# Two channel pieces placed earlier, and three ScalarE steps reordered, in a fused attention and Fourier-mix kernel

## The chip, the cores and the metric

The kernel runs on one core of a Trainium2 chip. A core has five engines with a queue each: TensorE (PE, matmuls and transposes, with its weight loads shown as PEld), VectorE (DVE), ScalarE (ACT), GpSimd (POOL) and SyncE (SP, which here only starts DMA transfers). Each engine works through its own instructions in the order in which the program gives them; engines wait for one another by semaphores. The metric is the device time of one execution in microseconds (us); lower is better.

## The reference

Two blocks follow one another. The first is an attention with a threshold, over 8 batches and 8 heads of 576 rows with 64 columns; the second mixes with a two-dimensional Fourier transform and ends in a normalised two-layer product.

```
scores = (q @ k.T) / 8
thresh = max(scores, rows) - tau
scores = where(scores >= thresh, scores, -1e9)
attn   = exp(scores - max) / (sum + 1e-9)
x      = (attn @ v), heads side by side: (8, 576, 512)
u      = x + real(fft over rows and columns of x)
un     = (u - mean(u)) / sqrt(var(u) + 1e-6)
out    = u + relu(un @ w_ch1) @ w_ch2        # 512 -> 2048 -> 512
```

The weights `w_ch1` and `w_ch2` arrive as 64-bit floats and are converted to 32 bits on the core.

## The kernel before, in words

**Steps.** A pair of heads is handled in five steps, four with 128 query rows of both heads and a fifth with the last 64 rows of both. With four pairs in a batch that gives 20 steps in a batch and 160 in all. They are numbered here from 0; step `i` belongs to pair `n = i // 5` and has `t = i % 5`. Steps 0 to 19 are the first batch (`step`, L1499), steps 20 to 39 the second (`second_batch`, L1647), and one loop runs steps 40 to 159 (L1724 on). All of it is unrolled, and the order of the program is written out by hand: what is called first is queued first on its engine.

**What a step does.** `scores(i)` puts the scores of 128 rows into PSUM: eight matmul records, at L440, or four at L446 in the fifth step of a pair. `softmax(i)` takes the row maxima (DVE, L461), the exponentials (ACT, L469), the threshold (ACT, L473), applies the threshold and sums (DVE, L477), and forms the inverse sums (`inverse`, DVE, L385 and L388). There are two score buffers, so the scores of step `i + 1` wait for the threshold operation of step `i`. `transposed_weights(i - 1)` transposes the weights of the step before on TensorE (L587, L590, L605), and ACT copies them from PSUM (L593 or L597, then L607 or L609). In the first two batches the inverse sums are not multiplied into the weights: `spread_inverse(i)` lets ACT spread them over 128 columns as `rec` (L509; in the fifth step of a pair a small copy, L504, comes first), TensorE transposes `rec` along with the weights (L590), and they are applied to the product with the values. `weighted_values` is that product (L636), twice per pair: in the second batch its first part is in the steps with `t = 2` and its second part in the steps with `t = 0` of the next pair. `scale_q` (ACT, L399) scales the queries of the next pair in the steps with `t = 2`, and `prep_pair` (DVE, L408 to L411) transposes queries and keys in the steps with `t = 3`, after which SP loads the next ones.

**Conversion.** `convert` turns 64-bit weights into 32-bit ones in stages spread over two steps: DVE (L296, L299), ACT (L304, L307), DVE (L311), POOL (L316), ACT (L318) and POOL (L319). The first batch converts `w_ch1`, the second `w_ch2` after the table `PLAN`, up to two pieces in a step.

**Channel work.** The two-layer product is done in groups of 512 rows. Group 0 is `channels`: 16 pieces of the first layer (each eight matmul records into one PSUM bank at L902, then a Relu, on ACT at L907 for an even piece and on DVE at L909 for an odd one), four loads of rows with their statistics (`rows.load`, L851 to L863), and then the second layer, four blocks of 16 matmuls each (L926) that is given out two matmuls at a time. `rows.factors()` takes the square roots (L874) and then a dummy exponential (L877), so that ACT loads its table of functions twice. Every two matmuls of the second layer also move on `w1_forms`, which stores pieces of `w_ch1` to memory (SP) and combines them (DVE, L970).

**The budget.** `fill()` is called three times in a step. Each call adds `per_slot` to `budget` and then runs pieces as long as `spent < budget`; every piece reports its cost in columns. `start_batch(0)`, in step 20, sets

```
keep = 4 * BT * NJ * DM // 128 if b == 0 else 3 * 7 * 2048
per_slot = (todo - spent - keep) / (3 * per_batch)
```

`keep` is what is left for the third batch: here 4 * 512 * 16 * 512 / 128 = 131072 columns. `todo` is 19240 for the mixing of the first batch and 264192 for group 0, so `per_slot` is 2539.3. In steps 23 to 39 the order of the program is: scores, softmax, `fill`, transposes of the step before, the ACT stage of the conversion, `fill`, `prep_pair` if due, `fill`, product with the values if due, `scale_q` if due, `spread_inverse`.

**PSUM.** All of these banks but the scores' come from one ring of four, tag `mm`; a new tile waits for the last reader of the bank that it is given.

Of the kernel before, what the change touches and what calls it, by code (L numbers as in the profile page):

```python
# [28 lines left out]
def _repeated(ap, n):  # L29

    return bass.AP(
        tensor=ap.tensor,
        offset=ap.offset,
        ap=[list(ap.ap[0]), list(ap.ap[1]), [0, n]],
    )
# [12 lines left out]
def kernel(  # L48
# [14 lines left out]
    DM = H * D  # L63
# [5 lines left out]
    NJ = HID // 128  # L69
# [7 lines left out]
    BT = 512  # L77
# [318 lines left out]
    def scale_q(n):  # L396

        raw = loaded[n][0]
        nc.scalar.activation(out=raw[:, :], in_=raw[:, :], func=ACT.Copy, scale=q_scale[:, :])  # L399
# [101 lines left out]
    def spread_inverse(i):  # L501
        e, den = steps[i]
        if i % NT == 4:
            nc.scalar.copy(e[:, S : S + 64], e[:, 512:S])  # L504
        if den is None:
            return
        nh = den.shape[1]
        rec = sb.tile([128, 2 * D], FP32, tag="rec", name="rec")
        nc.scalar.copy(  # L509
            rec[:, :].rearrange("p (j d) -> p j d", j=nh), _repeated(den, 2 * D // nh)  # L510
        )
        steps[i] = (e, rec)
# [44 lines left out]
    def transposed_weights(i):  # L557
        for _ in weights_in_parts(i):
            pass
# [337 lines left out]
    def channels(rows):  # L897
        for j in range(NJ):
            ht = hs[:, BT * j : BT * (j + 1)]
            ph = ps.tile([128, 512], FP32, tag="mm", bufs=4, name="ph")  # L900
            for c in range(ND):
                nc.tensor.matmul(  # L902
                    ph[:, :], w1[c][:, 128 * j : 128 * (j + 1)], u_t[:, c, 0:BT],
                    start=(c == 0), stop=(c == ND - 1),
                )
            if j % 2 == 0:
                nc.scalar.activation(out=ht, in_=ph[:, :], func=ACT.Relu)  # L907
            else:
                nc.vector.tensor_relu(ht, ph[:, :])  # L909
            yield 4 * ND * BT  # L910
            if j % 3 == 2 and j // 3 < 4:
                rows.load(j // 3)
                yield ND * 128
            if j == 12:
                rows.factors()
        def both():
            yield from w1_forms()
            ensure(1)
            while not next(forms_w2):
                yield  # L920

        forms = both()
        for t in range(4):
            po = ps.tile([128, DM], FP32, tag="mm", bufs=4, name="po")
            for j in range(NJ):
                nc.tensor.matmul(  # L926
                    po[:, :], hs[:, BT * j + 128 * t : BT * j + 128 * (t + 1)], w2[j],
                    start=(j == 0), stop=(j == NJ - 1),
                )
                if j % 2 == 1 and j < NJ - 1:  # L930
                    next(forms, None)
                    yield 2 * 4 * DM
            rows.add(t, slice(0, DM), po[:, :])
            rows.store(t)
            background()
            yield 2 * 4 * DM
        for _ in forms:
            pass
# [122 lines left out]
    def ensure(n):  # L1061

        nonlocal issued
        while issued <= n and issued < len(ALL_LOADS):
            src, count, k = ALL_LOADS[issued]
            n_blocks = min(PER, count - k)
            nc.sync.dma_start(
                out=w1[issued % 3][:, 0 : 512 * n_blocks].rearrange("p (j n) -> p j n", n=512),
                in_=src[:, k : k + n_blocks, :],
            )  # L1070
            issued += 1
# [367 lines left out]
    wanted = []  # L1439
# [59 lines left out]
    def step(i):  # L1499

        n, t = divmod(i, NT)
        scores(i)

        def stages(count):
            for _ in range(count if i - 1 in chunks else 0):
                next(chunks[i - 1], None)

        def next_stages():
            if i in chunks:
                next(chunks[i])  # L1510
            stages(2)

        def last_stage():
            stages(1)
            chunks.pop(i - 1, None)

        if t == 1 and n > 0:
            softmax(i, values_in_parts(n - 1, 1), next_stages, last_stage)
            load_v(n + 1)
        elif t == 3:  # L1520
            softmax(i, values_in_parts(n, 0), next_stages, last_stage)
        else:
            softmax(i, None, next_stages, last_stage)
        if t == 1 and n > 0:
            pass
        elif later and later[0][0] <= i:
            later.pop(0)[1](i)
        else:
            busy(2 if i < NCHUNK else 1)
        if t == 2:  # L1530
            scale_q(n + 1)
        if t == 3:
            prep_pair(n + 1)
        if t == 1:
            prep_ends(n)
        if i > 0:
            transposed_weights(i - 1)
        if i in chunks:
            next(chunks[i])
        while after and after[0][0] <= i:  # L1540
            after.pop(0)[1]()
        if i > 0 and i + 3 < NCHUNK:
            chunks[i + 3] = w1_chunk(i + 3)
        if t == 2 and n > 0:
            folds.append(fold_rows(n - 1))
        if folds and next(folds[0], True):
            folds.pop(0)
        spread_inverse(i)
        if i == 5:
            copy_seq()  # L1550
        if i == per_batch - 4:
            fold_halves(0)
        if i >= per_batch - 4:
            next(dim_copies)
# [54 lines left out]
    def advance(at):  # L1609
        for run in chunks.get(at, ()):  # L1610
            next(run, None)
# [10 lines left out]
    def start_batch(b):  # L1622

        nonlocal groups, todo, per_slot, budget
        mixes.append(mixing(b))
        todo += MIX
        while groups < NG and BT * (groups + 1) <= (b + 1) * S:
            rows = Rows(groups)
            work.append((b, channels(rows) if groups == 0 else two_level(groups, rows), rows))
            todo += cost(groups)  # L1630
            groups += 1

        keep = 4 * BT * NJ * DM // 128 if b == 0 else 3 * 7 * 2048
        per_slot = (todo - spent - keep) / (3 * per_batch)
        budget = spent

# [10 lines left out]
    def second_batch(i):  # L1647

        nonlocal budget
        n, t = divmod(i, NT)  # L1650
        first = i - per_batch
        if first > 0:
            transfers(first)
        if first != 1:
            scores(i)
        if first == 0:

            transposed_weights(i - 1)
        softmax(
            i, None, lambda: (advance(first), advance(first - 1), advance(first - 1)),  # L1660
            lambda: advance(first - 1),
        )
        chunks.pop(first - 1, None)
        if first == 0:
            transfers(first)
        fold_more()
        if first == 0:
            weighted_values(n - 1, 1)
            scores(i + 1)
            column_means(LAST)  # L1670
            copy_mean(LAST)
            folds.append(fold_rows(n - 1))
            while folds:
                fold_more()
            load_v(n + 1)
            start_batch(0)
            mix(3)
            mix(3)
        elif first == 1:
            mix(3)  # L1680
            transposed_weights(i - 1)
            mix(2)
            mirrored(LAST)
            for c, eng in ((1, nc.vector), (3, nc.vector), (0, nc.gpsimd), (2, nc.gpsimd)):
                less_mean(eng, LAST, c)
            advance(first)
        elif first == 2:
            mix(2)
            transposed_weights(i - 1)
            mix(2)  # L1690
            weighted_values(n, 0)
            advance(first)
        else:
            fill()
            transposed_weights(i - 1)
            advance(first)
            fill()
            if t == 3:
                prep_pair(n + 1)
            fill()  # L1700
            if t == 2:
                weighted_values(n, 0)
            if t == 0:
                weighted_values(n - 1, 1)
                folds.append(fold_rows(n - 1))
                load_v(n + 1)
        if t == 1:
            prep_ends(n)
        if t == 2:
            scale_q(n + 1)  # L1710
        if first == 16:
            fold_halves(1)
        if first < 3:
            budget += 3 * per_slot
        spread_inverse(i)

    for i in range(per_batch, 2 * per_batch):
        second_batch(i)
# [5 lines left out]
    for i in range(2 * per_batch, total):  # L1724


        n, t = divmod(i, NT)
# [149 lines left out]
```

## Time and profile before

| | us |
|---|---|
| median of 3 runs | 1574.14 |
| lowest and highest | 1572.99, 1577.97 |
| the profiled execution, its own time | 1571.58 |
| the span of its core | 1569.8 |
| steps 0 to 19 | 0 to 127.7 |
| steps 20 to 22 (mixing of the first batch) | 127.7 to 151.8 |
| steps 23 to 39 | 151.8 to 276.7 |

The page gives for each engine the time that it is busy, then the span in 40 slices of 39 us, and then the chain of work that ended last. Of the chain 83% is TensorE. The slices that matter here are the first seven, steps 0 to 39: TensorE is busy to 8 or 9 tenths there and to 9 tenths or more in each later slice. A view of the idle time of one engine names the instruction that waited and the one that released it; a timeline gives the instructions in order, with the idle time in square brackets. A wait counts only if nothing else of that engine could have run; TensorE works in order, so each of its waits is a stop of the whole queue.

The starts of the scores mark the steps. For steps 23 to 40 they are 151.76, 162.77, 168.36, 178.30, 184.15, 193.08, 198.65, 206.44, 215.60, 221.49, 233.61, 239.37, 244.97, 253.66, 259.51, 268.79, 274.55 and 276.70 us.

### The profile page before, as it was taken

How to read it: one execution, taken by the hardware profiler on the slowest of the kernel's cores; microseconds unless marked ns; L12 is line 12 of the kernel's file. 1: busy time of each engine (PE TensorE's matmuls, PEld its weight loads, DVE VectorE, ACT ScalarE, POOL GpSimd, SP SyncE). 2: the span in 40 equal slices, each digit the busy share in tenths (PEclk: the TensorE clock that was granted, in tenths of full speed). 3: DMA queues.
4: the chain of work that ended last, by engine and by line, in shares of the span. 5: the costliest groups of instructions: out<-in, count | busy, mean ns of one | idle time of the engine just before them, and what ended most of it. 6: DMA issues, size and time to landing. Idle time of an engine off the chain costs nothing.

```text
span 1569.8 us, 27001 instructions
## 1 busy us (share of the span) xinstructions
PE 1526.0 (97%) x9786; PEld 1187.1 (76%) x9786; DVE 1061.6 (68%) x2119; ACT 916.4 (58%) x1921; POOL 777.5 (50%) x962
## 2 busy tenths in 40 slices
PE   8988989999999999999999999999999999999999
PEld 4555545556788778877787778877787878889999
DVE  7987776846869566776577566866577666745546
ACT  6875666554666666656766566657666666232231
POOL 3774553034455652546254724555264625546735
PEclk9999999999999999999999999999999999999999
DMA  6423231646956264634454345635464434646655
GB/s 166 130 58 117 77 90 24 204 147 180 323 154 214 73 188 122 185 111 144 144 173 149 116 135 153 184 103 158 130 185 137 141 118 149 222 141 235 235 201 182
DMA packets 248907, 239.31 MB, mean 152 GB/s; under 512 B 197027, under 2 KB 218533, under 8 KB 228678
## 3 DMA queue, kind: packets, MB, share of 16 engines
q1 hardware_dynamic: 246262, 237.28, 49.6%
q8 instruction: 78, 1.28, 0.3%
q10 hardware_dynamic: 2512, 0.30, 0.1%
q14 instruction: 55, 0.45, 0.1%
HBM read 205.93 MB, written 31.46 MB: 151 GB/s over the span
## 4 chain that ended last, share of the span: by engine, by line
PE 83%; DVE 9%; ACT 4%; issue 1%; DMA 1%; POOL 1%; SPq 0%; ACTq 0%; DVEq 0%
PE ph L1203 24%; PE po L1390 18%; PE pv L636 9%; PE sc L440 9%; PE pw L605 7%; PE po L926 4%; PE ph L902 3%; PE sc L446 2%; PE py L759 2%; PE pa L776 1%; PE pe L587 1%; DVE neg L461 1%; PE pn L851 1%; PE pa L780 1%; PE pd L111 1%
## 5 line engine op out<-in xcount | busy, mean ns | idle before, releaser
L520 DVE TENSOR_REDUCE neg<-sc 128x1 f32<-128x576 f32 x216 | 154.3, 751 | 131.4 <-PE sc L440 118.6
L526 ACT ACTIVATE e<-sc,neg 128x576 f32<-128x576 f32 x216 | 158.5, 734 | 120.7 <-DVE neg L520 120.7
L1390 PE MATMUL po<-w,w_all 128*128 128x128 f32 x1728 | 219.0, 277 | 0.3 <-ACT ends L593 0.3
L1140 DVE TENSOR_TENSOR hs<-ph,hs 128x512 f32<-128x512 f32 (+1 forms) x128 | 105.4, 823 | 161.1 <-PE ph L1203 104.0
L1390 PEld LDWEIGHTS po<-w,w_all 128*128 128x128 f32 x1728 | 204.9, 192 | 9.2 <-issue 6.2
L1149 POOL TENSOR_TENSOR w<-hs 128x512 f32<-128x512 f32 x32 | 42.1, 1320 | 317.8 <-ACT hs L1145 243.9
L540 DVE SCALAR_TENSOR_TENSOR e<-sc,thr,e 128x576 f32<-128x576 f32 x216 | 168.4, 813 | 19.9 <-ACT thr L530 19.6
L1203 PE MATMUL ph<-u_t,w 128*128 128x256 f32 x768 | 180.5, 382 | 0.6 <-DMA w<-f 0.4
L607 ACT COPY e_t<-pw 128x512 f32<-128x512 f32 x256 | 148.7, 595 | 45.8 <-PE pw L605 44.7
L605 PE MATMUL pw<-ident,e 128*128 128x128 f32 x1152 | 169.9, 275 | 5.6 <-ACT ends L593 2.2
L440 PE MATMUL sc<-kT,qT 64*128 64x288 f32 x1024 | 168.1, 431 | 6.6 <-DVE e L477 4.4
L549 ACT ACTIVATE e<-e,den 128x576 f32<-128x576 f32 x216 | 157.5, 775 | 8.5 <-DVE den L388 7.7
L1203 PEld LDWEIGHTS ph<-u_t,w 128*128 128x128 f32 x768 | 141.4, 190 | 23.2 <-issue 4.4
L1203 PE MATMUL ph<-w_all,w 128*128 128x256 f32 x672 | 157.1, 383 | 1.1 <-DVE w_all L1125 1.0
L605 PEld LDWEIGHTS pw<-ident,e 128*128 128x128 f32 x1152 | 135.4, 141 | 21.9 <-issue 5.6
L1203 PEld LDWEIGHTS ph<-w_all,w 128*128 128x128 f32 x672 | 123.6, 190 | 23.7 <-issue 4.9
L1145 ACT ACTIVATE hs<-hs 128x512 f32<-128x512 f32 (+1 forms) x96 | 74.1, 771 | 113.5 <-DVE hs L1140 112.8
L440 PEld LDWEIGHTS sc<-kT,qT 64*128 64x128 f32 x1024 | 95.7, 187 | 57.9 <-issue 26.8
L1255 POOL TENSOR_TENSOR w_all<-w_all 128x128 f32<-128x128 f32 (+2 forms) x160 | 116.9, 747 | 30.3 <-DVE w_all L1410 22.4
L1390 PE MATMUL po<-w,hs 128*128 128x128 f32 x912 | 119.4, 278 | 0.3 <-ACT ends L593 0.3
L1390 PEld LDWEIGHTS po<-w,hs 128*128 128x128 f32 x912 | 109.7, 192 | 9.7 <-issue 7.1
L801 POOL TENSOR_TENSOR u_t<-x,tmp 128x289 f32<-128x289 f32 (+1 forms) x45 | 33.9, 753 | 123.7 <-DVE tmp L796 123.7
(224 smaller groups left out, 2946.7 us busy)
## 6 DMA issues: line engine op xcount, KB each, us to landing
w<-f SPq DMA_DIRECT2D x150, 1024.0 KB, 4.9
hs<-in_moe_w_ch_dram SPq DMA_DIRECT2D x23, 512.0 KB, 5.2
q_in<-in_q_dram SPq DMA_DIRECT2D x128, 72.0 KB, 4.1
out_dram<-u SPq DMA_DIRECT2D x36, 256.0 KB, 2.3
k_in<-in_k_dram SPq DMA_DIRECT2D x124, 72.0 KB, 2.6
v_in<-in_v_dram SPq DMA_DIRECT2D x64, 128.0 KB, 5.0
f<-w SPq DMA_DIRECT2D x14, 512.0 KB, 3.9
f<-w SPq DMA_DIRECT2D x7, 1024.0 KB, 4.8
```

What stands on the lines that cost most here:

```text
L440: nc.tensor.matmul(sc[j][:, c, 0:HALF], qT[hp, 128 * t : 128 * t + 128], kT[hp, k0 + HALF * c : k0 + HALF * (c + 1)], start=True, stop=True,)
L520: nc.vector.tensor_reduce(out=neg[:, j : j + 1], in_=sc[j][:, :, 0:HALF], axis=AXIS_XY, op=ALU.max, negate=True,)
L526: nc.scalar.activation(out=ej, in_=sc[j][:, :, 0:HALF], func=ACT.Exp, bias=neg[:, j : j + 1], scale=1.0)
L540: nc.vector.scalar_tensor_tensor(out=ej, in0=sc[j][:, :, 0:HALF], scalar=thr[:, j : j + 1], in1=ej, op0=ALU.is_ge, op1=ALU.mult, accum_out ...
L549: nc.scalar.activation(out=e[:, S * j : S * (j + 1)], in_=e[:, S * j : S * (j + 1)], func=ACT.Copy, scale=den[:, j : j + 1],)
L605: nc.tensor.transpose(pw[:, c, :], e[:, c0 : c0 + 128], ident[:, :])
L607: nc.scalar.copy(e_t[:, 4 * j : 4 * j + 4, qs], pw[:, :, :])
L636: nc.tensor.matmul(pv[64 * j : 64 * j + 64, 0:m], vt[:, 2 * c + j, :], e_t[:, 4 * j + c, 0:m] if c < 4 else ends[:, 0, 0:m], start=(c == 0 ...
L1140: nc.vector.tensor_tensor(out=to, in0=bank, in1=to if other is None else other, op=ALU.add)
L1203: nc.tensor.matmul(bank[:, 256 * q : 256 * q + 256].rearrange("p (two n) -> p two n", two=2), left[:, 256 * c + 128 * q : 256 * c + 128 * ...
L1255: return lambda: eng.tensor_tensor(out=to, in0=to, in1=other, op=ALU.add)
L1390: nc.tensor.matmul(to, lefts[m][j][:, s], right_[:, 128 * s : 128 * (s + 1)], start=jn in (0, 4) and s == 0, stop=s == 3, skip_group_check ...
```

## The change

Four things. `keep` for the first budget is smaller by two of 16 parts (114688 columns in place of 131072), so that `per_slot` in the second batch grows. The square roots of group 0 are no longer taken behind piece 12 of its first layer; after piece 15 the rows are put on the list `wanted`, which the loop of steps 40 on takes up behind the third stage of its softmax. In the first batch `spread_inverse(i)` is called right behind the transposes of the step before, and `scale_q` comes behind it, where it was ahead of the transposes. In steps 23 to 39 `spread_inverse(i)` is called right behind the transposes too, ahead of the ACT stage of the conversion and of two of the three `fill` calls; in steps 20 to 22 it stays at the end.

```diff
@@ channels
             if j % 3 == 2 and j // 3 < 4:
                 rows.load(j // 3)
                 yield ND * 128
-            if j == 12:
-                rows.factors()
+            if j == NJ - 1:
+                wanted.append(rows)
@@ step
-        if t == 2:
-            scale_q(n + 1)
         if t == 3:
             prep_pair(n + 1)
         if t == 1:
             prep_ends(n)
         if i > 0:
             transposed_weights(i - 1)
+        spread_inverse(i)
+        if t == 2:
+            scale_q(n + 1)
         if i in chunks:
             next(chunks[i])
...
-        spread_inverse(i)
@@ start_batch
-        keep = 4 * BT * NJ * DM // 128 if b == 0 else 3 * 7 * 2048
+        keep = 4 * BT * (NJ - 2) * DM // 128 if b == 0 else 3 * 7 * 2048
@@ second_batch
         else:
             fill()
             transposed_weights(i - 1)
+            spread_inverse(i)
             advance(first)
             fill()
...
         if first < 3:
             budget += 3 * per_slot
-        spread_inverse(i)
+            spread_inverse(i)
```

## The prediction

> **What bounds the kernel now.** I read the page first: total, engines, slices.
>
> ```profile
> span 1569.8 us, 27001 instructions
> PE 1526.0 (97%) x9786; PEld 1187.1 (76%) x9786; DVE 1061.6 (68%) x2119; ACT 916.4 (58%) x1921; POOL 777.5 (50%) x962
> PE   8988989999999999999999999999999999999999
> ```
>
> TensorE is the bound nearly everywhere. The change moves matmuls and removes none, so it can only win TensorE time that is idle or slow. Second, the two stretches between which work moves:
>
> ```profile
> core 0: us, PE busy (x) PEld busy (x) DVE busy (x) ACT busy (x) POOL busy (x), PEclk, DMA share, GB/s
> 151.76:276.70 124.94, 114.59 (x544) 63.67 (x542) 88.18 (x200) 84.15 (x190) 62.77 (x75) 0.99 0.24 60
> 276.70:480.00 203.30, 201.20 (x1091) 137.31 (x1092) 137.82 (x269) 113.66 (x234) 78.66 (x90) 1.00 0.68 206
> ```
>
> Steps 23 to 39 leave TensorE idle for 10.4 us, the third batch for 2.1. So work taken from the third batch shortens it by its full length. Third, what those 10.4 us wait for (window 151 to 280, TensorE alone):
>
> ```profile
> PE sc L446 <- DVE e L477: 3.1, 1, 3.1
> PE pe L590 <- ACT rec L509: 2.7, 3, 1.5
> PE ph L902 <- POOL u_t L805: 1.5, 1, 1.5
> PE sc L440 <- DVE e L477: 1.4, 1, 1.4
> PE ph L902 <- ACT ends L593: 1.2, 1, 1.2
> PE pe L587 <- ACT e L504: 1.1, 1, 1.1
> PE pv L636 <- ACT e_t L609: 0.8, 1, 0.8
> ```
>
> The first row is step 28, the fourth the border of steps 39 and 40: the two steps of 24 to 39 without a piece of channel work. The timeline of TensorE at step 28:
>
> ```profile
> 194.53 1.04 PE L605 MATMUL pw<-ident,e 128*128 128x128 f32 x8
> 198.65 1.85 PE L446 MATMUL sc<-kT,q_ends 128*128 128x288 f32 x4 [3.08 <-DVE e L477]
> 200.29 1.06 PE L851 MATMUL pn<-ident,u_t 128*128 128x128 f32 x4
> 201.14 4.27 PE L902 MATMUL ph<-u_t,w 128*128 128x512 f32 x8
> ```
>
> After the gap everything is slow: 1.85 us for scores that take 1.13 in step 24, 4.27 for a piece that takes 3.60. Windows of 1 us give a granted clock of 0.54, 0.50, 0.50 and 0.76 from 199 to 203, so 1.70 us more are lost. The same happens in the first batch at 82.94, after a gap of 2.17 us (0.51, 0.50, 0.50, 0.78: 1.71 us). Gaps of 1.5 us (steps 23 and 32) left the clock at 1.00.
>
> [...]
>
> **The change part by part.**
>
> *Budget.* `per_slot` becomes (19240 + 264192 - 114688) / 60 = 2812.4 in place of 2539.3. Over 60 calls that is 16384 columns: four outputs of the second layer at 4096, two matmuls each. A piece of 8192 columns takes 3.53 us from start to start of what follows (step 26, 180.62 to 184.15), so 16384 are 7.06 us. I stepped both budgets through the calls. Before: pieces 2 to 5 come in the third call of steps 24 to 27, none in 28, piece 6 in the first call of 29, then one in each step to 38, from 32 on in the second or third call; none in 39. The trace has them there. After: piece 2 in step 24 up to piece 15 in step 37, always in the first call, ahead of the transposes; then two outputs each in 38 and 39. So 7.06 us enter steps 23 to 39 and leave the third batch, and the loads of rows move with their pieces.
>
> *Waits that go.* Step 28: 3.08 idle and 1.70 of slow clock, covered by piece 6 and a load (4.0 us). Steps 39 and 40: the eight score records of step 40 lie from 276.70 to 280.00, where they take 1.17 otherwise, so 2.13. Waits for `rec` and its copy: 1.09 (step 25), 0.25 (27), 1.52 (32), 0.91 (37); a piece now stands between the scores and these transposes, and `rec` is ready meanwhile. The 1.19 of step 32 (the piece waits for a bank behind four transposes) goes, since that load is in step 31. Sum 11.9 us.
>
> *Waits that come.* A product with the values used to have a piece between it and the transposes it reads. Now it follows them directly in steps 25, 27, 32, 35 and 37, and waits for the last copy. Step 30 is so already: 0.80, which stays. I take 0.9 each for steps 25, 27, 35 and 37 and 1.9 for 32, where ACT has 2.3 us of conversion from step 31 (four at 0.53 to 0.61) ahead of its exponentials, two signs (1.1) and the Relu of piece 10 (0.5) ahead of the copies: 5.5 us. To check, I set steps 23 to 40 out engine by engine in program order with the spacings of the timelines: the order of before meets all starts of the scores within 0.35 us, the new order ends the scores of step 40 about 0.4 us earlier than before with the 7.06 us done. So 6.4 by the waits, up to 7.5 by the layout; I take 6.4.
>
> *Square roots.* They leave step 36, where they hold `rec` back:
>
> ```profile
> 258.58 1.28 ACT L874 ACT_TABLE_LOAD   x1
> ...
> 260.18 1.28 ACT L877 ACT_TABLE_LOAD   x1
> ...
> 261.58 0.28 ACT L509 COPY rec<-den 128x128 f32<-128x128 f32 x1
> ```
>
> That is the 0.91 counted above. They go to step 40, 3.0 us behind its softmax. ACT idles 1.54 us there (to 286.41); the exponentials of step 41 come 1.5 late, while the threshold of step 41 waits on DVE to 290.05, 2.1 after them. Nothing; if that cover is gone, 1.5.
>
> *Copies of the inverse sums, second batch.* In the layout the order alone changes no start of scores: `rec` is needed a step later. Nothing, between -0.5 and +0.5.
>
> *First batch.* In step 12 the scaling of the queries stands ahead of the copy that frees a bank:
>
> ```profile
> 81.83 0.79 ACT L399 ACTIVATE q_in<-q_in,q_scale 128x576 f32<-128x576 f32 x1
> 82.50 0.38 ACT L593 COPY ends<-pe 128x256 f32<-128x256 f32 x1
> ```
>
> Without it the gap of 2.17 becomes 1.5, which did not slow the clock elsewhere: 0.67 and 1.71. Not all stays: ACT still has scaling and conversion (1.8) ahead of the exponentials of step 13, which begin at 86.5, not 87.06, by my count. Against it, in step 2 `rec` waits for the sums (ready at 26.47, copies done at 25.55) with the conversion behind it: at most 0.9, and DVE, busy to 29.35, hides most. I take -0.8, between -2.3 and +0.9.
>
> *Queues.* With two outputs begun in step 38, six stores of 512 KB from `w1_forms` are issued ahead of `prep_pair(8)` on SP instead of behind it. They wait for nothing, SP is idle from 255 to 275, and the five combinations on DVE (1.22 us at L970) in steps 39 and 40 lie where DVE waits 1 to 3 us a step. Nothing; up to 1 if the stores hold up the next queries.
>
> **Sum.** -6.4 - 0.8 = -7.2 us. The profiled execution took 1571.58 (span 1569.8), so 1564.4; the median of the runs shown is 2.56 higher, so 1566.9.
>
> **The rivals.** *A, the forecast,* 1566.9; its own range is 1563.5 to 1570.
>
> *B, a bank turns a wait around.* In step 27 the product of the values may get the bank of piece 5. Its Relu is on DVE behind the sums, and these wait for a transfer of weights (DVE starts at 188.80 after 1.96 idle, the sums end at 192.85). Then the product starts about 2.8 us late, the clock halves (1.7), and the layout ends step 40 3.8 us later than in A: -3.4 in all, 1570.7. For it: four banks, five uses. Against it: in step 30, where the odd piece 7 stands ahead, the next uses in the program take the banks of the transposes first.
>
> *C, the third batch does not shrink.* If loads or DVE bound it, the 7.06 us come back as waits: 1574. Against it: 2.1 us idle in 203.
>
> *D, slower: ACT becomes the loop.* In steps 28 to 33 the Relu of a piece now stands ahead of the copies, `rec` and the conversion, and all of it ahead of the next exponentials. If ACT sets the pace there, the gaps are not filled, only moved: 7.06 added and 5.5 of waits, 7.06 saved, and the removed waits come back as waits for exponentials: about +5, 1579. It decides if the exponentials of these steps start over 1.5 us behind their maxima; I count 0 to 1.8, the latter in 32 alone. Against it: ACT is busy 84 of 125 us.
>
> **How the numbers follow.** 0.3% of this time is 4.7 us, about what a measurement can tell from no change. A 0.62, B 0.20, C 0.07, D 0.11. Faster by more than that: most of A and a third of B, 0.66. Within it: the rest of A and B, and C: 0.23. Slower: D, 0.11. The range is 1562.5 (A with the upper ends of layout and first batch, and a little) to 1574.5 (B and C inside, D left out).
>
> **What would show it.** No gap at step 28 and the clock at 1.00 from 190 to 210; pieces directly behind the scores in steps 24 to 37; waits of 0.8 to 1.9 us for L607 or L609 at the products; steps 40 and on starting within 1 us of before; the third batch 7 us shorter; table loads in step 40. Wrong: a wait of the product of step 27 for DVE, half a clock at new places, or a third batch as long as before.

## The result, and the profile after

| | before | after |
|---|---|---|
| median of 20 runs each, us | 1573.73 | 1569.99 |
| lowest and highest | 1570.55, 1577.97 | 1564.76, 1574.36 |
| ratio, 95% interval | | 0.9977 [0.9967, 0.9987] |
| the profiled execution, its own time | 1571.58 | 1569.68 |

3.7 us are gained (2.0 to 5.2 by the interval), 0.23%: the forecast was 7.2 us and had the right sign and about twice the size. The two profiles differ by 1.9 us only, since the profiled execution of before was 2.2 us under its median and that of after 0.3.

The page of after, total and engines and slices:

```profile
span 1567.9 us, 27009 instructions
PE 1526.6 (97%) x9786; PEld 1186.7 (76%) x9786; DVE 1058.1 (67%) x2119; ACT 918.4 (59%) x1921; POOL 772.8 (49%) x962
PE   8998999999999999999999999999999999999999
```

The same stretches as before, in the windows view:

```profile
core 0: us, PE busy (x) PEld busy (x) DVE busy (x) ACT busy (x) POOL busy (x), PEclk, DMA share, GB/s
151.76:276.70 124.94, 119.04 (x551) 65.66 (x551) 88.06 (x203) 83.45 (x190) 60.45 (x73) 1.00 0.34 89
276.70:480.00 203.30, 199.17 (x1092) 137.37 (x1094) 136.31 (x266) 113.77 (x231) 76.10 (x92) 0.99 0.63 194
```

TensorE idles 5.9 us in steps 23 to 39 where it idled 10.4, as intended. But in the third batch it idles 4.1 where it idled 2.1, and its mean clock is 0.99 there: something was gained in the first stretch and given back in the second.

To see where, I put the starts of the scores of both profiles side by side, step by step, and add the channel work that is already done more than before, at 3.53 us for 8192 columns. The **lead** is then what has been gained so far. (Step 21 starts at 127.70 us in before by this count, step 20 at 121.18.)

| at the start of step | 21 | 41 | 50 | 53 | 54 | 55 | 57 | 62 |
|---|---|---|---|---|---|---|---|---|
| lead, us | 1.90 | 9.36 | 9.34 | 7.77 | 7.91 | 3.33 | 2.75 | 2.40 |

Steps 23 to 40 gained 7.46 us, the upper value of the prediction. Nothing happens until step 50. Then 6.9 us are lost by step 62, 4.6 of them in step 54. These are TensorE's waits in after, window 365 to 455 (engine, what waited, what it waited for; total, times, longest):

```profile
PE ph L1203 <- DVE hs L1140: 2.7, 4, 1.6
PE pe L587 <- ACT e L549: 1.2, 1, 1.2
```

Step 54 on the timeline of TensorE (start, duration, idle time before in brackets):

```profile
408.59 1.21 PE L446 MATMUL sc<-kT,q_ends 128*128 128x288 f32 x4
409.63 1.89 PE L1203 MATMUL ph<-u_t,w 128*128 128x256 f32 x8
412.69 0.33 PE L587 MATMUL pe<-ident,e 128*128 128x128 f32 x1 [1.16 <-ACT e L549]
...
415.00 3.31 PE L1203 MATMUL ph<-t_u,w 128*128 128x256 f32 x8 [1.55 <-DVE hs L1140]
```

and the granted clock behind it (windows of 2 us; the clock is the third number from the right):

```profile
414.00:416.00 2.00, 1.00 (x4) 0.84 (x5) 2.00 (x4) 1.62 (x5) 0.38 (x1) 0.88 0.57 158
416.00:418.00 2.00, 2.00 (x6) 1.54 (x5) 0.60 (x4) 0.47 (x1) 1.30 (x3) 0.50 0.18 70
418.00:420.00 2.00, 2.00 (x10) 1.78 (x9) 0.00 (x0) 1.43 (x3) 0.00 (x0) 0.77 1.05 397
```

TensorE is idle for 1.16 and 1.55 us, and loses 0.24 + 1.0 + 0.46 = 1.7 us by the slow clock: 4.4 of the 4.6. The weights of step 53, for which it waits first, come late. The exponentials are ready at 400.96, when ScalarE ends this:

```profile
400.23 0.73 ACT L526 ACTIVATE e<-sc,neg 128x576 f32<-128x576 f32 x1
```

VectorE shows why the weights are late all the same:

```profile
399.90 0.87 DVE L1002 TENSOR_TENSOR w<-w_all,w 128x512 f32<-128x512 f32 x1
403.97 1.23 DVE L1140 TENSOR_TENSOR hs<-ph,hs 128x1024 f32<-128x1024 f32 x1 [3.20 <-PE pe L587]
405.11 2.59 DVE L1002 TENSOR_TENSOR w_all<-w_all 128x512 f32<-128x512 f32 x2
407.63 0.81 DVE L540 SCALAR_TENSOR_TENSOR e<-sc,thr,e 128x576 f32<-128x576 f32 x1
```

and GpSimd beside it:

```profile
403.51 1.48 POOL L718 TENSOR_TENSOR sums<-f 128x608 f32<-128x608 f32 x1
405.07 1.49 POOL L719 TENSOR_TENSOR f<-f 128x608 f32<-128x608 f32 x1
```

L540 is the threshold of step 53. It starts at 407.63, 6.7 us behind its exponentials, because two things stand ahead of it in VectorE's queue. One is the 128x1024 add of a piece (L1140), which waits 3.20 us for TensorE to reach that piece. The pieces of this group are products, seven in a part, numbered in the order 1, 2, 5, 6, 4, 7, 3; this is product 7. The other is two subtractions of the weights' forms (L1002, sums and differences of blocks of `w_ch2`), which take 2.59 us where two of the same size take 1.28 at 410.07. In before the exponentials of step 53 were ready at 406.54, and the threshold was 0.17 us late:

```profile
405.51 1.28 DVE L1002 TENSOR_TENSOR w_all<-w_all 128x512 f32<-128x512 f32 x2
406.71 0.81 DVE L540 SCALAR_TENSOR_TENSOR e<-sc,thr,e 128x576 f32<-128x576 f32 x1
```

The add is there by an accident of numbers. The third batch fills three slots a step, the first of them ahead of the threshold. When it takes its budget, in step 42, 20480 columns more are done than in before (five pieces of 4096: four in steps 38 and 39, a fifth by the end of step 41), so that the budget is 4792.1 columns a slot (5133.5 before). Six slots are 28752 columns, and seven pieces of 4096 are 28672. So the pattern repeats every two steps, and in steps 51, 53, 55 and 57 the first slot gets the same two pieces: product 4 and product 7.

### The profile page after: what moved, and what is told of

Read it like the earlier page. It is cut to its first block, busy times and chain, and to the rows that moved or that the text cites. A ratio compares the mean times of both kernels' runs of the same rounds, so it can differ in the third digit from the quotient of the medians.

```text
span 1567.9 us, 27009 instructions
## 1 busy us (share of the span) xinstructions
PE 1526.6 (97%) x9786; PEld 1186.7 (76%) x9786; DVE 1058.1 (67%) x2119; ACT 918.4 (59%) x1921; POOL 772.8 (49%) x962
## 3 DMA queue, kind: packets, MB, share of 16 engines
q8 instruction: 78, 1.28, 0.3%
## 4 chain that ended last, share of the span: by engine, by line
PE 84%; DVE 9%; ACT 3%; issue 1%; POOL 1%; DMA 0%; POOLq 0%; ACTq 0%; DVEq 0%
PE ph L1203 24%; PE po L1390 18%; PE pv L636 9%; PE sc L440 9%; PE pw L605 7%; PE po L926 4%; PE ph L902 3%; PE sc L446 2%; PE py L759 2%; PE pa L776 1%; PE pe L587 1%; PE pn L851 1%; PE pa L780 1%; PE po L1369 1%; DVE f L740 1%
## 5 line engine op out<-in xcount | busy, mean ns | idle before, releaser
L1140 DVE TENSOR_TENSOR hs<-ph,hs 128x512 f32<-128x512 f32 (+1 forms) x128 | 105.3, 822 | 169.3 <-PE ph L1203 97.4
L1149 POOL TENSOR_TENSOR w<-hs 128x512 f32<-128x512 f32 x32 | 42.0, 1315 | 316.5 <-ACT hs L1145 242.5
L540 DVE SCALAR_TENSOR_TENSOR e<-sc,thr,e 128x576 f32<-128x576 f32 x216 | 168.2, 811 | 19.0 <-ACT thr L530 18.9
L593 ACT COPY ends<-pe 128x128 f32<-128x128 f32 (+1 forms) x128 | 38.1, 298 | 64.0 <-PE pe L587 41.7
```

The costliest lines, as they stand in the source:

```text
L540: nc.vector.scalar_tensor_tensor(out=ej, in0=sc[j][:, :, 0:HALF], scalar=thr[:, j : j + 1], in1=ej, op0=ALU.is_ge, op1=ALU.mult, accum_out ...
L1140: nc.vector.tensor_tensor(out=to, in0=bank, in1=to if other is None else other, op=ALU.add)
```

## The experiments

All are compared with the kernel before. The leads are from one profile each, by the same reckoning as above. n is the number of timed runs, and the clock is the granted clock of TensorE, the mean over these runs; in the runs of before that were timed beside the experiments it is 0.9943 to 0.9948. A difference of 0.001 I take as at most 1.6 us of time, an estimate (0.001 of 1570 us).

| run | n | clock | ratio, 95% | lead at 21 | at 41 | at 50 | at 62 | lost from 50 to 62 |
|---|---|---|---|---|---|---|---|---|
| after | 20 | 0.9962 | 0.9977 [0.9967, 0.9987] | 1.90 | 9.36 | 9.34 | 2.40 | 6.9 |
| step only | 21 | 0.9935 | 1.0001 [0.9993, 1.0009] | 1.49 | 1.47 | 1.46 | 1.77 | -0.3 |
| rest only | 13 | 0.9956 | 0.9987 [0.9976, 0.9999] | 0.86 | 8.25 | 8.23 | -0.04 | 8.3 |
| keep only | 14 | 0.9951 | 1.0003 [0.9989, 1.0017] | 0.79 | 4.34 | 4.31 | -0.92 | 5.2 |
| copy back | 22 | 0.9962 | 0.9978 [0.9967, 0.9988] | 1.87 | 9.31 | 9.29 | 2.24 | 7.1 |
| add behind | 5 | 0.9970 | 0.9957 [0.9945, 0.9970] | 1.69 | 9.12 | 9.09 | 5.44 | 3.7 |
| add behind, all | 5 | 0.9976 | 0.9961 [0.9949, 0.9973] | 2.96 | 10.38 | 10.36 | 7.05 | 3.3 |
| forms behind | 22 | 0.9947 | 1.0008 [1.0001, 1.0016] | 2.69 | 10.10 | 10.09 | -1.13 | 11.2 |
| add and forms | 13 | 0.9957 | 0.9994 [0.9984, 1.0004] | 2.91 | 10.31 | 10.29 | 1.35 | 8.9 |
| fold later | 5 | 0.9972 | 0.9962 [0.9948, 0.9976] | 1.73 | 9.18 | 9.16 | 2.46 | 6.7 |
| piece later | 21 | 0.9959 | 0.9983 [0.9976, 0.9990] | 0.11 | 7.51 | 7.46 | 3.36 | 4.1 |
| quarter piece | 14 | 0.9945 | 1.0002 [0.9990, 1.0013] | 0.48 | 7.92 | 7.88 | 1.38 | 6.5 |
| both | 14 | 0.9960 | 1.0005 [0.9993, 1.0017] | 0.67 | 8.12 | 8.09 | 1.62 | 6.5 |

### The parts of the change

**The first batch's step alone.** The kernel before, with only

```diff
-        if t == 2:
-            scale_q(n + 1)
...
         if i > 0:
             transposed_weights(i - 1)
+        spread_inverse(i)
+        if t == 2:
+            scale_q(n + 1)
...
-        spread_inverse(i)
```

> The kernel before with only the reordering of the first batch's step (copy of the inverse sums behind the weights' copies, scaling of the queries behind that). Theory: the whole first-batch part comes from here and nothing else, so the starts of the scores are 1.9 us earlier than before from step 14 on and stay so to the end: ratio 0.9988, about 1571.8 us. Rival: the shift is given back where the third batch's own order is fixed by something else, so ratio 1.000.

The ratio is 1.0001: the 1.9 us that the pair of profiles showed were not the edit's alone. What lead there is stays to step 62 (1.77), so it is not given back in the third batch either. From step 12 to step 20 the lead of this profile grows by 0.57 us. The gap of step 12 is 1.93 us, where it was 2.17, and the slow clock behind it is still there (0.61 and 0.54 in 82 to 86). In after the gap is 1.91 us, and the slow clock is gone. In the eleven profiles with this order the lead changes by +2.2, +0.6 or +0.5, and once by -1.1 us, between these steps: values about 1.6 apart, the size of one such stretch of slow clock. On average it gains 1.1; in the two other profiles with the old order it loses 0.1 and 0.2. The timed interval goes from 1.1 us faster to 1.4 slower, so a gain of 1 us lies at its edge. The mean clock of its runs is 0.0008 under that of the runs of before beside it, up to 1.3 us, which can hide such a gain.

**All but that step.** After, with the step of the first batch as before.

> The changed kernel with the step of the first batch put back as before: only the two pieces, their factors and the copy in the second batch's step are new. Theory: about 7.5 us are gained by step 41, and most is lost in steps 51 to 57, where the 128x1024 add of a piece stands ahead of the threshold of the step; what is left is 0.5 to 1.5 us: ratio 0.9990 to 0.9997, and the loss in step 54 is there with nothing of the first batch's shift. Rival: the loss comes from the first batch's 1.9 us moving transfers against the second half of the weights' forms; then this kernel keeps its 7.5 us: ratio 0.995.

The profile is as the theory has it: 7.4 us are gained from step 21 to 41 and lost from 50 on, 5.9 of it in step 54, at the same two instructions and with the same two waits (1.2 and 1.6). It is more than the 4.6 of after because the slow clock behind them lasts twice as long here (6.8 us for 3.4). The first batch has no part in the loss. The timed gain, 2.0 us, is a little above what was expected.

**The smaller reserve alone.** Before, with `NJ - 2` in `keep` and nothing else.

> The kernel before with the smaller reserve alone (14 chunks for 16): factors after the thirteenth chunk, copies in both batches and the first batch's step as before. Theory: the other edits are worth nothing, so ratio 0.9987 as in the run without the first batch's step, with the loss in step 54. Rival: the square roots ahead of the last three chunks in the second batch change ScalarE's table twice in a place where a softmax waits: 1.5 to 3 us slower than that, 0.9997 to 1.0006.

The rival holds. Up to step 35 as much is gained as in the others, then 4.3 us go in that step. ScalarE there:

```profile
245.94 0.71 ACT L318 ACTIVATE stage<-stage 128x512 f32<-128x512 int32 x1
246.66 1.28 ACT L874 ACT_TABLE_LOAD   x1
...
248.26 1.28 ACT L877 ACT_TABLE_LOAD   x1
...
250.20 0.59 ACT L609 COPY e_t<-pw 128x512 f32<-128x512 f32 x1
```

and TensorE:

```profile
250.84 4.01 PE L636 MATMUL pv<-e_t,v_in 128*64 128x320 f32 x16 [3.02 <-ACT e_t L609]
```

The square roots now stand in the first slot, ahead of the weights' copies, and the product behind them waits 3.02 us and then takes 4.01 us, where the same product takes 2.38 in before and in after. With the old reserve they came in the third slot and cost the 0.91 that the prediction counted. So moving them is worth 0.9 us by itself by that count (no run has it alone), but some 4 us to the smaller reserve, which gains 3.55 us from step 21 to 41 where after gains 7.46: the edits don't add.

**The copy of the second batch put back.**

```diff
             transposed_weights(i - 1)
-            spread_inverse(i)
             advance(first)
...
-            spread_inverse(i)
+        spread_inverse(i)
```

> The changed kernel with the copy of the inverse sums put back to the end of the second batch's step. Theory: worth nothing (0.5 us either way), so ratio 0.9972 to 0.9982 as for the changed kernel, and steps 23 to 41 within 0.3 us of it. Rival: the copy behind the weights' copies carries part of the 7.5 us gained by step 41, then 1 us or more of the lead is gone there.

The copy is worth nothing: 7.44 us are gained from step 21 to 41 without it, 7.46 with it.

### The loss in the third batch

**The add behind the threshold.** After, with this in `two_level`:

```diff
                 elif m == 7:
...
-                    add(both, twice)
-                    relu(both)
+                    if not (g == 1 and holding):
+                        add(both, twice)
+                        relu(both)
...
                 tick()
+                if m == 7 and g == 1 and holding:
+                    held.append(lambda to=both, x=twice: (add(to, x), relu(to)))
```

> The changed kernel, every piece in its slot, but the 128x1024 add of product 7 and its ReLU issued behind the threshold when the piece falls into the slot ahead of it (second group of channels alone, so steps 51, 53, 55 and 57). Theory of the add that stands ahead of the threshold: TensorE's waits of 1.16 and 1.55 us in step 54 and the half clock behind them go, 4 to 5.5 us are kept: ratio to the kernel before 0.9940 to 0.9955. Rival (the forms' 2.6 us on VectorE are what delays the threshold, or the third batch cannot shrink): at most 1 us better than the changed kernel, ratio 0.9970 to 0.9977.

VectorE in step 53 of this kernel:

```profile
401.82 1.87 DVE L1002 TENSOR_TENSOR w_all<-w_all 128x512 f32<-128x512 f32 x2
403.61 0.81 DVE L540 SCALAR_TENSOR_TENSOR e<-sc,thr,e 128x576 f32<-128x576 f32 x1
```

The subtractions no longer wait behind the add and run before GpSimd's two folds, beside smaller instructions of it (1.87 us), and the threshold starts 1.5 us behind its exponentials (402.10), not 6.7. No wait of TensorE in window 365 to 455 is over 0.6 us, the clock is 1.00 throughout, and 3.3 us less are lost than in after. The ratio, 0.9957, lies just beside what the theory expected and clear of the rival. The same order in every group (`g == 1` left out):

> Product 7's add behind the threshold in every group of channels, not in the second alone. Theory: only the second group pays for it, since TensorE waits 0.3 us in all for that add after 455 us in the changed kernel; ratio the same as with the second group alone, 0.9957 within 0.001. Rival: the same order costs in every later group through late softmaxes, then 2 us or more better: 0.9945 or less.

It brings no more: 0.9961, and 3.3 us lost. The medians of the two are 1567.55 and 1567.08 us, under those of both kernels of the case, though of five runs each.

**The forms behind the threshold.** After, the add where it was, but

```diff
-                next(forms, None)
+                if not holding:
+                    next(forms, None)
```

> The changed kernel with product 7's add left ahead of the threshold, but no step of the weights' forms in that slot. Theory that the add's wait for TensorE decides: the threshold of step 53 still waits until the add ends at 405.2, instead of 407.6; the wait of 1.16 us goes, the 1.55 us may stay, and the half clock goes with the first: 2 to 4 us better than the changed kernel, 0.9950 to 0.9965. Rival A, the add alone decides: 0.9975. Rival B, the forms alone decide: as good as with the add moved, 0.9957, and no TensorE idle over 0.6 us in 404 to 420.

In step 54 it comes near to rival B: the longest wait is 0.75 us, and the lead at step 57 is 7.8, so that 2.3 of it are lost where after had lost 6.6. But the ratio is 1.0008, which none of the three expected, because the forms end too late for the second half of the group. The store of the last one is issued at 446.54, and a sum on GpSimd that waits for it (L1149) starts at 451.62; in after three of its four parts were done by 439.6. TensorE, window 365 to 470:

```profile
PE po L1391 <- POOL w_all L1184: 3.0, 1, 3.0
PE po L1391 <- DMA w<-f: 2.6, 1, 2.6
```

8.6 us are lost in step 58. With the add moved as well it is the same, with 6.6 in that step, and the expectation is missed again (0.9994):

> The kernel with product 7's add behind the threshold, and besides this no step of the weights' forms taken in the slot ahead of the threshold: the same forms come in the other slots. Theory: what is left of the loss in steps 51 to 57 (2.6 us of TensorE idle in 368 to 440) is VectorE being late with adds behind the forms, so 0.5 to 2 us more: ratio 0.9940 to 0.9955. Rival: the forms' stores come later and TensorE waits for their loads, or the late adds are not due to the forms: 0.9955 to 0.9970.

So in the slots of after either of the two, out of the way, frees step 54, but the forms have a deadline of their own.

**The fold later.** After, with GpSimd's two instructions put off by one call:

```diff
         if n % NPAIR == 1 and b > 1:
+            if b == 2:
+                yield
             fold_halves(b)
```

> The changed kernel with GpSimd's two fold instructions of the third batch's second pair (L718 and L719, 1.5 us each) put off to the next place where a fold is continued, about a step later. Theory that they slow the two form subtractions beside them (2.59 us in step 53, 1.28 elsewhere): these take 1.3 us there, the threshold of step 53 ends about 1.2 us earlier, TensorE's wait of 1.16 us for the weights goes, and with it the half clock, if the folds do not meet VectorE's next forms: 2 to 4 us better than the changed kernel, 0.9950 to 0.9965. Rival A (the stretch is not due to GpSimd): the row stays at 2.5 us and the ratio at 0.9977. Rival B: the stretch goes, but VectorE is slowed a step later and TensorE waits 1.5 us for product 7's add as before: 0.9970 to 0.9980.

VectorE in step 53, two lines further down in the file by the edit:

```profile
405.29 1.28 DVE L1004 TENSOR_TENSOR w_all<-w_all 128x512 f32<-128x512 f32 x2
406.50 0.81 DVE L540 SCALAR_TENSOR_TENSOR e<-sc,thr,e 128x576 f32<-128x576 f32 x1
```

and TensorE:

```profile
411.56 0.33 PE L587 MATMUL pe<-ident,e 128*128 128x128 f32 x1 [0.20 <-ACT e L549]
414.94 2.69 PE L1205 MATMUL ph<-t_u,w 128*128 128x256 f32 x8 [2.61 <-DVE hs L1142]
```

By the profile this is rival B. The longer time of the subtractions was GpSimd's doing: 2.59 becomes 1.28, and the first wait becomes 0.20. But the folds now lie at 411.59 to 414.95 beside VectorE's next work, the second wait grows from 1.55 to 2.61, the clock is 0.57 in 416 to 420 (0.50 and 0.77 in after), and 6.7 us are lost for 6.9. The timed ratio, 0.9962, looks better than that; it rests on five runs, its interval overlaps that of after, and of the 6 us up to 3.8 go with the clock (0.9972 for 0.9948). It also warns that 0.9957 against 0.9977 is not by itself proof for the runs with the add behind, of which up to 4.2 of 6.8 us go with the clock too: there the profile carries the claim, here it contradicts it.

**Other places for the pieces.** The third batch begins one piece later (`budget = spent - 4096` for b == 1):

> The changed kernel with the third batch's channel work one piece (4096 columns) later; nothing is added or left out. Theory of the place: the budget of 4792 columns a slot, six slots in two steps, is 28752, nearly seven pieces of 4096, so in every second step the same pair (products 4 and 7) falls into the slot ahead of the threshold and the threshold waits behind the 128x1024 add of product 7. One piece later the pair is products 6 and 4, whose last needs no add: the loss of steps 51 to 57 goes, the lead of 9.4 us is kept to within 2.5 us, ratio to the kernel before 0.9940 to 0.9960, about 1565 to 1567 us. Rival (the weights' forms on VectorE and the folds on GpSimd slow each other wherever the pieces lie, and the third batch cannot shrink): ratio as for the changed kernel, 0.9975.

This is half right. The pair is now 6 and 4, and 4.1 us are lost by step 62 for 6.9, though step 54 still has waits of 1.01 and 1.47 us. But step 63 loses 3.4 more, where the mixing of the next batch, moved against its neighbours, has TensorE wait:

```profile
503.62 0.49 PE L759 MATMUL py<-dim_c,f 128*128 128x128 f32 x2 [2.94 <-DVE f L740]
```

Before and after wait 1.2 us there. A quarter of a piece earlier (`+ 1024`), so that product 7 comes alone:

> The changed kernel with the third batch's channel work a quarter of a piece (1024 columns) earlier, worked out so that the slots from step 62 on hold the same pieces as in the changed kernel. The pair of products 4 and 7 is parted: product 7 stands alone in the slot ahead of the threshold in steps 51 to 57. Theory of the pair: the add then waits for one product and no longer for two, the threshold of step 53 ends 1.7 to 2 us earlier, TensorE's wait in step 54 and the half clock go: ratio 0.9950 to 0.9965. Rival (one product's wait and the forms' 2.6 us are enough to make the threshold late): 0.9970 to 0.9980.

The theory of the pair fell. The add waits 0.71 us for TensorE, no longer 3.20. Yet the threshold starts 4.7 us behind its exponentials (ready at 405.70), because the subtractions now lie beside the folds with their whole length:

```profile
406.57 3.90 DVE L1002 TENSOR_TENSOR w_all<-w_all 128x512 f32<-128x512 f32 x2
410.39 0.80 DVE L540 SCALAR_TENSOR_TENSOR e<-sc,thr,e 128x576 f32<-128x576 f32 x1
```

and on GpSimd:

```profile
406.58 1.47 POOL L718 TENSOR_TENSOR sums<-f 128x608 f32<-128x608 f32 x1
408.12 1.80 POOL L719 TENSOR_TENSOR f<-f 128x608 f32<-128x608 f32 x1
```

Both waits of step 54 are there (1.16 and 1.55), with one more of 1.18 for the scores, this time at a clock of 1.00. The ratio, 1.0002, is worse than either side expected: step 63 costs 2.5 us more, with a wait of 2.02 at the place that piece later showed, though the slots there hold the same pieces as in after. With the add behind the threshold too, in every group:

> Product 7's add behind the threshold in every group, and the quarter piece earlier. Theory: both take away the same loss, so together no more than the better of the two: 0.9950 to 0.9965. Rival: the pair in the slot costs by its own length too (the later products of the step are held up behind two pieces), then 0.5 to 1.5 us more: 0.9945 to 0.9952.

Both waits of step 54 go, but 6.5 us are lost as without the move: the pieces now wait elsewhere for L1140, 4.0 us in all with 1.1 at the longest, and step 63 again costs 2.5. So the repair by the add belongs to the slots as they fall in after; it is no cure for any other phase.

## Why the prediction was half right

- **Steps 23 to 40: right, at the upper end.** 7.46 us were gained, for 6.4 by the waits and 7.5 by the layout. The gap of step 28 is gone. The waits that come were over-estimated: at the products of steps 25, 27, 32, 35 and 37 they are 0.79, 0.33, 1.17, 0.79 and 0.24, 3.3 us in all for 5.5. Of the two estimates the engine-by-engine layout was the better one, and I took the other.
- **Rival B fell.** The product of step 27 waits 0.33 us, and not for the bank. **Rival D fell** too: no loop of ScalarE shows, the lead grows.
- **Square roots: right** that step 40 hides them (lead 9.36 at step 41, 9.41 at 42). What I did not see is that leaving them would have cost some 4 us and not 0.91 in the new slots; since they were moved, the sum is not touched.
- **Copies of the second batch: right**, nothing. **First batch: -0.8 to within what can be told**; the profiles give a gain of 1.1 on average over a range of 3.3, the timed run anything from 1.1 faster to 1.4 slower. The gap of step 12 became 1.9 us in all eleven profiles, not 1.5, and in four of them the clock fell behind it (to 0.61 and 0.54 in step only): that a gap of 1.5 us had left the clock alone elsewhere was no ground for counting on it here.
- **The third batch: wrong, and this is the miss of the sum.** "So work taken from the third batch shortens it by its full length" reckoned 7.06 us from 2.1 us of idle time in 203. The work did go; 6.9 us came back in steps 50 to 61, of which 3.4 us are more idle time and 1.7 half a clock. It is the outcome of rival C, to which I gave 0.07, by a cause that I had not named: no engine or load is the bound there, but the change of the budget moves every later piece to another slot, and the new pattern puts the add of product 7 and the forms ahead of one threshold and the folds beside them. That is shown for step 54: taking out the add or the forms takes away its loss. I stepped the new budget through steps 23 to 39 and stopped there; the same stepping to step 57 would have shown the pair.
- **The number: in part luck.** By the profiles 7.46 us are gained and 6.9 lost again, which leaves 0.5, and the first batch's 1 us; timed are 3.7. The granted clock tells where most of the rest lies. Its mean is 0.9962 in the runs of after and 0.9943 to 0.9948 in those of before: 2.2 to 3.0 us by an estimate (0.0014 to 0.0019 of 1570 us), which is an upper one: in step 83 of after some 1.7 us of clock go with 1.16 us of time. So 1 to 2 us of the gain are less waiting. The pair of profiles agrees: of the lead of 2.40 at step 62, 1.7 is one slow stretch less (two up to there in after, three in before). The sum had the clock at steps 12 and 28 alone, and not what came in step 54; which stretches the timed runs are without, no record shows.
- **What is not settled.** With the add behind, 3.3 to 3.7 us are still lost in steps 50 to 62, and no order that was tried loses less. TensorE idles 2.6 us there in 368 to 440 (0.5 in before), in waits of 0.3 to 0.6 for adds and copies. Behind each of these six waits the next matmul starts 0.16 us later than the idle time and the usual spacing give, which is close to 1 us more; what is left, under 1 us, I can't place.

## What to carry to other kernels

Where work is dealt out by a budget per slot, a change of the budget is an edit to every later slot: step the dealing through to the end of the stretch, and look at which piece falls ahead of each instruction that others wait for, above all where a whole number of slots comes near a whole number of pieces. Idle time of 1% in a stretch says that nothing is wrong in the present order, not that work taken from it is saved. Two edits of which each is worth little may need each other, as the reserve and the square roots do here. And where two kernels differ by a few tenths of a per cent, compare the granted clock of their runs before the time is put down to the schedule.

## What the runs showed of the hardware

**The same gap halves the clock or not.** In step 83, where this change alters nothing, before has gaps of 1.51 and 0.70 us 1.3 us apart, and its clock stays at 1.00; after has 1.51 and 0.59 at the same two instructions and the clock falls to 0.73, 0.50 and 0.91 in 674 to 680, some 1.7 us of clock; the step takes 13.10 us for 11.94. Before:

```profile
676.99 0.49 PE L759 MATMUL py<-dim_c,f 128*128 128x128 f32 x2 [1.51 <-DVE f L740]
678.28 0.66 PE L605 MATMUL pw<-ident,e 128*128 128x128 f32 x4 [0.70 <-DVE w_all L1410]
```

The same transposes in after:

```profile
675.88 1.11 PE L605 MATMUL pw<-ident,e 128*128 128x128 f32 x4 [0.59 <-DVE w_all L1410]
```

In the same way the gap of 1.9 us in step 12 halves the clock in four of eleven profiles: in step only it falls to 0.61 and 0.54 in 82 to 86, in fold later the scores behind the gap take 2.30 us, while in after they take 1.25 at a clock of 1.00. The waits of 1.16 and 1.55 us in step 54 halve it in after (0.50 in 416 to 418; the eight matmuls behind them take 3.31 us), but not in quarter piece, where sixteen such matmuls behind the same two waits take 3.72 us. What decides between the two outcomes no run here shows. Step 83 alone makes the two profiles differ by 1.16 us, and the slow stretch of step 12 in before is 1.71 us: this is why the first batch could not be read from one pair.

**Two subtractions take longer beside GpSimd's folds.** The same two subtractions of 128x512 take 1.28 us with GpSimd idle (fold later), 2.59 beside one fold (after) and 3.90 with both folds beside them (quarter piece). Each fold beside them adds 1.31 us; the folds themselves take 1.47 to 1.80 us there.
